# Six late experts of a mixture of experts: placed by index in 512-row units, or by token count in units of 352, 320 and 512 rows

## The chip, the cores and the metric

The kernel runs on one core of a Trainium2 chip. The metric is the device time of one execution in microseconds, as a median over runs.

## What is computed

Attention with a threshold, then a top-1 mixture of experts on its output. The attention of 8 batches and 8 heads over 576 positions gives 4608 tokens of 512 values. Each token goes to the one of 8 experts with the largest logit, and the expert's output is scaled by two gates:

```python
logits = x @ w_gate                      # x: (4608, 512), w_gate: (512, 8)
e_idx = np.argmax(logits, axis=1)
...
for e in range(E):
    mask = e_idx == e
    h = np.maximum(x[mask] @ w1[e], 0.0)  # w1[e]: (512, 1024)
    ye = h @ w2[e]                        # w2[e]: (1024, 512)
    out[mask] = gate_w[mask, None] * eom[mask, e, None] * ye
```

How many tokens each expert has is data. Counted from the reference on its own inputs, experts 0 to 7 have 619, 496, 677, 491, 670, 499, 508 and 648.

## The kernel before

**Attention** (`Attention`) runs first, with TensorE (PE), VectorE (DVE) and ScalarE (ACT) all near full. While it runs, `Router.route` finds the expert of each token, one batch pair at a time, and `Router.scatters` writes each token's row (512 values, its gate, its token number) to its place in the DRAM buffer `xs`, where every expert has a region of its own. The rows that units will read are filled beforehand from `zrow` (`init_units`), whose token number is out of range, so that an unused row writes nothing.

**The expert stage** (`Experts.run`) is a row of 12 units, written out at build time. A unit is a block of rows of one expert: experts 0 and 1 (the early ones) have 384 rows, which hold only tokens of the first three batch pairs, and run while the last batch pair is still being routed. Experts 2 to 7 (the late ones) have 512 rows each, and four `Pair` units of 256 rows stand between them for what is over. The order is E0, E1, E2, E3, pair, E4, pair, E5, pair, E6, pair, E7. Beside the fourth pair one tile of 128 rows (`Flex`) is computed, and whatever is still over goes through a loop at the end (`rest`), one tile of 128 rows at a time. Which expert a pair, the single tile and the loop's tiles take is found on chip: `Router.finish` counts what is over, and `table` makes `prows` (pairs) and `rows` (tiles), from which SP loads registers (`where`).

**Within a unit** each of 8 steps f does 12 matmuls of the first layer (`first`: weights stationary, the unit's N rows moving, lines 1065 to 1067, in three terms of a high and a low part) and then, one step behind, three matmuls for each tile of up to 128 rows in the second layer (`second`, `tile_step`: rows stationary, 512 columns of w2 moving, lines 1091 to 1093). ACT makes `hh` (line 1070) and DVE `hl` (line 1071) between the two. Weights come in chunks of two steps, four chunks for each unit; ACT and DVE split them (lines 858 and 861), and four raw buffers are refilled by SP as they come free (`load_next`).

**A unit's rows** are fetched by SP (`gather`, `fetch`, line 832) into `xg`, which has one buffer, then turned by DVE (line 1046), and split by ACT and DVE (lines 858 and 861) into `xh` and `xl`. For unit 2, the first late one, the gather has to wait for all rows of the last batch pair: its nine scatters, and then eight pad scatters (`finish`, line 698), all on GpSimd's queue (POOL, line 551), where the outputs are scattered too (line 849).

**What sets the order.** PE, DVE and ACT run in the order in which the program is written. The routing is a generator, and `rt.advance` takes it from one `yield` to the next at fixed places: four times in each step of unit 0, twice in each later step. In the expert stage POOL and SP get their order from a scheduler.

The lines of the routing that the change touches (648 to 671, then the loop of the nine scatters) are these:

```python
        nc.gpsimd.tensor_tensor(pso, pos, oh, op=ALU.mult)
        yield "V"
        split = bp <= self.cut and self.early
        dsti = t2("dsti", I32)
        V.tensor_reduce(dst, pso, axis=AX.X, op=ALU.add)
        ...
            V.tensor_copy(dsti, dst)
        ...
        for b in range(n):
```

Of the kernel before, what the change touches and what calls it, by code (L numbers as in the profile page):

```python
# [16 lines left out]
P = 128  # L17
# [434 lines left out]
class Router:  # L452
    NPAIR = 4

    def __init__(self, ctx, tc, ntok, E, DM, early, esize, cut):
# [4 lines left out]
        self.base = [esize if e < early else 4 * P for e in range(E)]  # L460
# [49 lines left out]
        self.prows = c.tile([1, 2, self.NPAIR], I32, name="pairs")  # L510
        self.total = c.tile([1, 1], I32, name="total")
# [15 lines left out]
    def init_units(self):  # L527
        E = self.E
        parts = [(self.xs[self.A :, :], "itok")]
        for e in range(self.early, E + 1):  # L530
            n = self.base[e] if e < E else 2 * P
            parts.append((self.xs[e * self.CAP : e * self.CAP + n, :], "itok"))
        for dst, group in parts:
            for r in range(0, dst.shape[0], P):
                ins = self.nc.sync.dma_start(dst[r : r + P, :], self.zrow)
                self.nodep(ins, group)
                self.behind(ins)
                self.init.append(ins)
                yield False
# [96 lines left out]
    def scatters(self, bp, rows, oh, sc, pr):  # L636
# [12 lines left out]
        yield "V"  # L649
        split = bp <= self.cut and self.early  # L650
# [35 lines left out]

    def finish(self, ctx):
# [16 lines left out]
        V.tensor_tensor(nf, self.cnt[0:1], self.ebase[0:1], op=ALU.subtract)  # L704
# [9 lines left out]
        yield from self.table(sm, "p", self.prows, cp, 2 * P, self.ebase[0:1])  # L714
# [5 lines left out]
        V.scalar_tensor_tensor(v, m0, float(2 * P), self.ebase[0:1], op0=ALU.mult, op1=ALU.add)  # L720
# [45 lines left out]
class Experts:  # L766
    RB, NW, YB = 4, 4, 4
    PAIRS = (2, 4, 6, 8)
# [56 lines left out]
    def fetch(self, xg, keys, src, after):  # L825
# [4 lines left out]
        parts.append((keys, src[:, self.rt.DM :].rearrange("(t p) w -> p t w", p=P)))  # L830
# [3 lines left out]
    def emit_out(self, y, keys, n):  # L834
        nc, DM = self.nc, self.rt.DM
        yo = self.yp.tile([P, DM], F32, name="yo")
        sc = keys[:, n, 0:1]
# [9 lines left out]
        else:  # L847
# [3 lines left out]
            out_offset=bass.IndirectOffsetOnAxis(ap=keys[:, n, 1:2].bitcast(I32), axis=0),  # L851
# [29 lines left out]
    def begin(self, nstatic):  # L881
        rt = self.rt
        make = [lambda e=e: Base(self, e) for e in range(rt.E)]
        for s, at in enumerate(self.PAIRS):
            make.insert(rt.early + at, lambda s=s: Pair(self, s))
# [7 lines left out]
        self.nload = self.done = self.used = 0  # L893
# [43 lines left out]
    def run(self):  # L937
        rt, nun = self.rt, len(self.make)
        prev, fin = None, False
        for i in range(nun):  # L940
            b, final = self.unit(i), i == nun - 1
            late = 4 if i == rt.early - 1 else 0
            for f in range(8):
# [17 lines left out]
                if not (final and f == 7):  # L961
                    if prev:
                        prev[0].second(prev[1], prev[0] is self.unit(nun - 1))
# [47 lines left out]
class Base:  # L1011
    def __init__(self, ex, e):
        self.ex, self.nc, self.e = ex, ex.nc, e
        self.nt = ex.rt.base[e] // P
        self.reset()

    def reset(self):
        self.N = self.nt * P
        self.Y, self.h, self.w = None, {}, {}

    def gather(self):
        ex, rt, e = self.ex, self.ex.rt, self.e
        early = e < rt.early
        r0 = rt.A + e * rt.esize if early else e * rt.CAP
        after = [x for g, x in rt.tok if g == "A" or not early]
        if not early:
            after += rt.pads
        else:
            assert sum(g == "A" for g, _ in rt.tok) == 9 * (rt.cut + 1)
# [54 lines left out]
    def tile_step(self, t, f, i):  # L1084
# [3 lines left out]
        n = Y.shape[1]  # L1088
        wh, wl = (w[:, f % 2, i * n : i * n + n] for w in (w2h, w2l))
        ts = slice(t * P, t * P + P)  # L1090
# [4 lines left out]
    def last(self, f0, f1):  # L1095
        for t, Y in enumerate(self.Y):
# [3 lines left out]
            self.ex.emit_out(Y, self.keys, t)  # L1100

    def finish(self):
        for t, Y in enumerate(self.Y):
            self.ex.emit_out(Y, self.keys, t)
# [9 lines left out]
class Pair(Base):  # L1114
    def __init__(self, ex, s):
        self.ex, self.nc = ex, ex.nc
        self.nt = 2
        assert "p" in ex.rt.tables
        self.e, self.row = where(ex, ex.rt.prows, s)
        self.reset()  # L1120

    def gather(self):
        rt = self.ex.rt
        self.fetch(rt.xs[bass.ds(self.row, self.N), :], [x for _, x in rt.tok] + rt.pads)

# [166 lines left out]
```

## Time and profile before

| | us |
|---|---|
| Median of 3 runs (909.41 to 909.97) | 909.64 |
| The profiled execution | 913.79 |
| Its span, first to last instruction | 912.1 |
| PE busy | 899.3 (99%) |
| DVE busy | 692.8 (76%) |
| ACT busy | 617.6 (68%) |
| POOL busy | 338.0 (37%) |
| Mean granted clock of TensorE | 0.999 of full speed |

The profile is of one execution, which was 4.15 us longer than the median run. Matmuls are pipelined: what the profile gives as the time of one is longer than the distance to the next, so a busy PE says nothing of its pace. The pace is read from the starts of matmuls that follow one another.

### The profile page before, as it was taken

How to read it: one execution, taken by the hardware profiler on the slowest of the kernel's cores; microseconds unless marked ns; L12 is line 12 of the kernel's file. 1: busy time of each engine (PE TensorE's matmuls, PEld its weight loads, DVE VectorE, ACT ScalarE, POOL GpSimd, SP SyncE). 2: the span in 40 equal slices, each digit the busy share in tenths (PEclk: the TensorE clock that was granted, in tenths of full speed). 3: DMA queues.
4: the chain of work that ended last, by engine and by line, in shares of the span. 5: the costliest groups of instructions: out<-in, count | busy, mean ns of one | idle time of the engine just before them, and what ended most of it. 6: DMA issues, size and time to landing. Idle time of an engine off the chain costs nothing.

```text
span 912.1 us, 22576 instructions
## 1 busy us (share of the span) xinstructions
PE 899.3 (99%) x8649; PEld 660.0 (72%) x8649; DVE 692.8 (76%) x1646; ACT 617.6 (68%) x1265; POOL 338.0 (37%) x529
## 2 busy tenths in 40 slices
PE   8999999999999999999999999999999999999997
PEld 4666666666666666666678978888888888888885
DVE  7999999999999999999987764545745645656821
ACT  6999999999999999999974343424434434435711
POOL 4354454656746577476656410101101101101101
PEclk9999999999999999999999999999999999999999
DMA  5477651333413334133258973527537537728401
GB/s 169 154 243 223 213 176 67 114 115 115 161 59 114 113 110 166 61 114 134 95 143 268 287 186 115 183 93 225 187 96 228 178 103 218 204 88 244 160 22 47
DMA packets 92206, 136.68 MB, mean 150 GB/s; under 512 B 14527, under 2 KB 61247, under 8 KB 92096
## 3 DMA queue, kind: packets, MB, share of 16 engines
q1 hardware_dynamic: 85456, 114.20, 41.0%
q0 software_dynamic: 6640, 21.02, 6.3%
q8 instruction: 68, 1.11, 0.5%
q14 instruction: 42, 0.34, 0.1%
HBM read 105.75 MB, written 30.22 MB: 149 GB/s over the span
## 4 chain that ended last, share of the span: by engine, by line
PE 88%; ACT 5%; DVE 3%; issue 2%; DMA 1%; another core or an unknown queue 0%; POOLq 0%; POOL 0%; DVEq 0%
PE ps L160 12%; PE pr L295 9%; PE pa L295 8%; PE ph L1066 7%; PE ph L1067 7%; PE ph L1065 7%; PE py L1093 7%; PE py L1091 7%; PE py L1092 7%; PE pt L263 7%; PE pa L221 3%; PE ps L157 2%; PE pa L321 2%; ACT p L176 2%; DMA xg<-xs 1%
## 5 line engine op out<-in xcount | busy, mean ns | idle before, releaser
L188 DVE SCALAR_TENSOR_TENSOR p<-s,thr,p 128x576 f32<-128x576 f32 x288 | 230.9, 838 | 0.0
L176 ACT ACTIVATE p<-s,mn 128x576 f32<-128x576 f32 x288 | 213.8, 783 | 24.5 <-DVE s L166 21.6
L166 DVE TENSOR_SCALAR_CACHE_REDUCE s<-ps 128x576 f32<-128x576 f32 x288 | 205.8, 751 | 26.0 <-PE ps L160 14.8
L1070 ACT ACTIVATE hh<-ph 128x512 fp32r<-128x512 f32 (+3 forms) x96 | 48.4, 504 | 189.5 <-PE ph L1067 181.1
L171 POOL TENSOR_SCALAR thr<-mn,tau_sb 128x2 f32<-128x2 f32 x144 | 107.3, 745 | 175.4 <-DVE s L166 174.6
L849 POOL DMA_INDIRECT out_dram<-yo,keys x38 | 40.5, 1065 | 353.6 <-DVE yo L848 186.0
L1071 DVE SCALAR_TENSOR_TENSOR hl<-ph,hh 128x512 fp32r<-128x512 f32 (+3 forms) x96 | 54.9, 572 | 130.5 <-ACT hh L1070 129.2
L160 PE MATMUL ps<-qk 64*128 64x288 f32 x1024 | 153.6, 419 | 0.2 <-DVE s L166 0.2
L1065 PE MATMUL ph<-xh,w1h 128*128 128x512 f32 (+2 forms) x380 | 132.1, 348 | 0.6 <-ACT xh L858 0.6
L1066 PE MATMUL ph<-xl,w1h 128*128 128x512 f32 (+2 forms) x380 | 131.8, 347 | 0.5 <-DVE xl L861 0.5
L1067 PE MATMUL ph<-xh,w1l 128*128 128x512 f32 (+2 forms) x380 | 131.9, 347 | 0.0
L1091 PE MATMUL py<-w2h,hh 128*128 128x512 f32 (+1 forms) x304 | 119.2, 392 | 0.0
L1092 PE MATMUL py<-w2l,hh 128*128 128x512 f32 (+1 forms) x304 | 118.6, 390 | 0.0
L1093 PE MATMUL py<-w2h,hl 128*128 128x512 f32 (+1 forms) x301 | 118.1, 392 | 0.0
L160 PEld LDWEIGHTS ps<-qk 64*128 64x128 f32 x1024 | 88.5, 190 | 16.2 <-DVE s L166 2.1
L295 PE MATMUL pr<-PTb,vld 128*64 128x320 f32 x640 | 100.0, 442 | 0.0
L263 PE MATMUL pt<-ident,p 64*128 64x64 f32 x2288 | 95.9, 223 | 0.2
L263 PEld LDWEIGHTS pt<-ident,p 64*128 64x128 f32 x2288 | 83.1, 139 | 2.6 <-ACT PTa L278 0.7
L295 PE MATMUL pa<-PTa,vld 128*64 128x256 f32 x640 | 80.3, 387 | 1.8 <-ACT PTb L246 1.1
L861 DVE TENSOR_TENSOR w1l<-r,w1h 128x1024 fp32r<-128x1024 f32 x52 | 64.0, 1231 | 20.9 <-ACT w1h L858 15.4
L1065 PEld LDWEIGHTS ph<-xh,w1h 128*128 128x128 f32 x380 | 71.4, 188 | 11.3 <-ACT xh L858 1.1
L1066 PEld LDWEIGHTS ph<-xl,w1h 128*128 128x128 f32 x380 | 71.5, 188 | 11.0 <-DVE xl L861 0.8
(225 smaller groups left out, 1500.6 us busy)
## 6 DMA issues: line engine op xcount, KB each, us to landing
r<-in_moe_w_dram SPq DMA_DIRECT2D x104, 512.0 KB
qk<-in_qkv_dram SPq DMA_DIRECT2D x31, 928.0 KB
vld<-in_qkv_dram SPq DMA_DIRECT2D x32, 320.0 KB
xs<-zrow SPq DMA_DIRECT2D x32, 257.0 KB
xg<-xs SPq DMA_DIRECT2D x24, 256.0 KB
xg<-xs SPq DMA_DIRECT2D x16, 128.0 KB
xg<-xs SPq DMA_DIRECT2D x8, 192.0 KB
out_dram<-yo,keys POOLq DMA_INDIRECT x38
```

What stands on the lines that cost most here:

```text
L160: nc.tensor.matmul(ps[x][:, cs], q, k, start=True, stop=True)
L166: nc.vector.tensor_scalar(s, ps[a][:, c0 : c0 + S], SC, None, op0=ALU.mult, op1=ALU.min, accum_out=mn[:, a : a + 1])
L176: self.nc.scalar.activation(e, ss[a], AF.Exp, bias=mn[:, a : a + 1], scale=-1.0)
L188: nc.vector.scalar_tensor_tensor(e, s, thr[:, a : a + 1], e, op0=ALU.is_le, op1=ALU.mult, accum_out=sums[a])
L263: nc.tensor.transpose(pt[:, o : o + 64], p[hs[h], k0 : k0 + P], id_[hs[h], hs[h]])
L295: nc.tensor.matmul(pa[self.half[a], 0:N], vm[:, kb, a], PT[:, 4 * a + kb if i else self.NK - 1], start=(i == 0), stop=(i == self.NB), skip ...
L1065: nc.tensor.matmul(ph, w1h[:, c, fs], self.xh[:, c, 0:N], start=(c == 0), stop=False)
L1066: nc.tensor.matmul(ph, w1h[:, c, fs], self.xl[:, c, 0:N], start=False, stop=False)
L1067: nc.tensor.matmul(ph, w1l[:, c, fs], self.xh[:, c, 0:N], start=False, stop=(c == 3))
L1091: nc.tensor.matmul(Y, hh[:, ts], wh, start=(f == 0), stop=False)
L1092: nc.tensor.matmul(Y, hh[:, ts], wl, start=False, stop=False)
L1093: nc.tensor.matmul(Y, hl[:, ts], wh, start=False, stop=(f == 7))
```

## The change

The base of the late experts is no longer an expert by its index but a slot by its rank. On chip, once the last batch pair is counted, the six late experts are ranked by their number of tokens (`Router.ranks`). The first has 704 rows, in two units of 352; the second and the third have 672 rows, in units of 352 and 320; the other three have one unit of 512 each. One `Pair` and the `Flex` tile remain for what is over, the two early experts' rows included. The row of units is E0, E1, 352, 352, 352, 320, 352, 320, 512, 512, pair, 512: twelve again, with 256 rows fewer. The nine late slots all take their expert and their row in `xs` from a new table `order` through registers, and no late weight is loaded before that table is there. A unit may now end in a tile of 96 or 64 rows.

```diff
 class Router:
-    NPAIR = 4
+    NPAIR = 1
+    SLOTS = ((352, 352), (352, 320), (352, 320), (512,), (512,), (512,))
...
         for dst, group in parts:
-            for r in range(0, dst.shape[0], P):
-                ins = self.nc.sync.dma_start(dst[r : r + P, :], self.zrow)
+            n = dst.shape[0]
+            m, a = (P, 1) if n % P == 0 else (n // 8, 2)
+            for r in range(0, n, m * a):
+                ins = self.nc.sync.dma_start(
+                    dst[r : r + m * a, :].rearrange("(a p) w -> p a w", a=a),
+                    self.zrow[0:m, None, :].broadcast_to([m, a, self.W]),
+                )
...
         nc.gpsimd.tensor_tensor(pso, pos, oh, op=ALU.mult)
         yield "V"
+        if bp == self.cut + 1:
+            yield from self.ranks()
         split = bp <= self.cut and self.early
         dsti = t2("dsti", I32)
         V.tensor_reduce(dst, pso, axis=AX.X, op=ALU.add)
...
+    def ranks(self):
+        nc, E, e0, V, sm = self.nc, self.E, self.early, self.nc.vector, self.small
...
+        V.scalar_tensor_tensor(key, self.cnt[0:1, e0:], float(E), key, op0=ALU.mult, op1=ALU.add)
+        V.tensor_tensor(cmp, across(key), down(key), op=ALU.is_gt)
+        yield False
+        V.tensor_reduce(rank, cmp, axis=AX.X, op=ALU.add)
...
+        V.scalar_tensor_tensor(tbl[:, 1], tbl[:, 0], float(self.CAP), off, op0=ALU.mult, op1=ALU.add)
+        V.tensor_copy(self.order, tbl)
+        self.tables.append("o")
+        yield False
...
-        V.tensor_tensor(nf, self.cnt[0:1], self.ebase[0:1], op=ALU.subtract)
+        V.tensor_tensor(nf, self.cnt[0:1], self.ends, op=ALU.subtract)
...
-        make = [lambda e=e: Base(self, e) for e in range(rt.E)]
-        for s, at in enumerate(self.PAIRS):
-            make.insert(rt.early + at, lambda s=s: Pair(self, s))
+        make = [lambda e=e: Base(self, e) for e in range(rt.early)]
+        for s, n in enumerate(n for x in rt.SLOTS for n in x):
+            make.append(lambda s=s, n=n: Slot(self, s, n))
+        make.insert(self.FLEX, lambda: Pair(self, 0))
...
     def load_next(self):
-        if self.nload < len(self.seq):
+        self.due += 1
+        while self.nload < min(self.due, len(self.seq)):
             i, g = self.seq[self.nload]
+            if i is not None and i >= self.rt.early and not self.rt.tables:
+                return
             self.nload += 1
             self.raws.append(self.load(self.unit(i).e, g))
...
         wh, wl = (w[:, f % 2, i * n : i * n + n] for w in (w2h, w2l))
-        ts = slice(t * P, t * P + P)
+        ts = slice(t * P, t * P + m)
```

**What moves, first place.** DVE in unit 0, from the copy of the last batch pair's prefix sums (`pr`) to the reduction that gives each row its place (`dst`, `dsti`). `hl` belongs to the unit's steps, `w1l` and `w2l` are weights being split. Before:

```order
L631 COPY pr<-px 128x80
L861 TENSOR_TENSOR w2l<-r_1637,w2h 128x1024
L652 TENSOR_REDUCE dst<-pso 128x9
L671 CAST dsti<-dst 128x9
L1071 SCALAR_TENSOR_TENSOR hl<-ph,hh 128x384
L861 TENSOR_TENSOR w1l<-r_8529,w1h 128x1024
L1071 SCALAR_TENSOR_TENSOR hl<-ph,hh 128x384
```

Now `pr` and `w2l` are followed by nine instructions of `ranks` (from `key` to `tbl`), and then by these:

```order
L1129 SCALAR_TENSOR_TENSOR hl<-ph,hh 128x384
L917 TENSOR_TENSOR w1l<-r_8531,w1h 128x1024
L728 SCALAR_TENSOR_TENSOR tbl<-tbl,off 1x9
L729 CAST order<-tbl 1x18
L732 TENSOR_TENSOR capr<-rank,asc 1x36
L733 TENSOR_TENSOR capr<-capr,caps 1x36
L735 COPY ends<-ebase 1x2
L736 TENSOR_REDUCE ends<-capr 1x6
L737 TENSOR_TENSOR ends<-ends,ecap 1x6
L664 TENSOR_REDUCE dst<-pso 128x9
L683 CAST dsti<-dst 128x9
L1129 SCALAR_TENSOR_TENSOR hl<-ph,hh 128x384
```

`dst` has moved behind one `hl`, one split of weights and sixteen small instructions of `ranks`.

**Second place.** POOL in units 0 and 1: the scatters of the last batch pair's rows (`xs<-rows`), the pads (`xs<-zrow`) and the outputs of unit 0 (`out_dram`). Before:

```order
L644 TENSOR_TENSOR pos<-pr,cc 128x72
L646 TENSOR_TENSOR cnt<-pr,cc 128x8
L648 TENSOR_TENSOR pso<-pos,pre_148 128x72
L551 DMA xs<-rows,dsti 38912x514 x9
L551 DMA xs<-zrow,padi 38912x514 x8
L849 DMA out_dram<-yo,keys 4608x512 x34
```

and now:

```order
L654 TENSOR_TENSOR pos<-pr,cc 128x72
L656 TENSOR_TENSOR cnt<-pr,cc 128x8
L658 TENSOR_TENSOR pso<-pos,pre_148 128x72
L561 DMA xs<-rows,dsti 38912x514 x9
L905 DMA out_dram<-yo,keys 4608x512 x3
L561 DMA xs<-zrow,padi 38912x514 x8
L905 DMA out_dram<-yo,keys 4608x512 x31
```

The three output scatters of unit 0 now stand ahead of the eight pads, for which unit 2's gather waits.

**Third place.** DVE in the first steps of unit 2, behind the weights that are split for its next steps. `ci`, `inas`, `v1s` belong to the table of single tiles (`finish`), `yo` is unit 1's output. Before, that table stood in unit 1, and these rows followed one another:

```order
L861 TENSOR_TENSOR w2l<-r_8972,w2h 128x1024
L1071 SCALAR_TENSOR_TENSOR hl<-ph,hh 128x512
L848 TENSOR_SCALAR yo<-py,keys 128x512 x2
L861 TENSOR_TENSOR w1l<-r_9099,w1h 128x1024
L1071 SCALAR_TENSOR_TENSOR hl<-ph,hh 128x512
```

and now:

```order
L917 TENSOR_TENSOR w2l<-r_8998,w2h 128x1024
L782 MEMSET ci 1x1
L784 TENSOR_TENSOR ci<-ci,nf 1x1 x6
L1129 SCALAR_TENSOR_TENSOR hl<-ph,hh 128x352
L904 TENSOR_SCALAR yo<-py,keys 128x512 x2
L917 TENSOR_TENSOR w1l<-r_9099,w1h 128x1024
L784 TENSOR_TENSOR ci<-ci,nf 1x1 x2
L776 CAST total<-ci 1x1
L799 TENSOR_TENSOR inas<-sid,ci 1x352
L800 TENSOR_TENSOR inbs<-sid,ci 1x352
L801 TENSOR_TENSOR inas<-inas,inbs 1x352
L803 TENSOR_SCALAR v1s<-ci 1x8
```

Two more rows of the table (`v1s`, `inbs`) follow before the second `hl` of unit 2.

## Rows read from the trace of the kernel before

**Rows 1.** The page's part 1: busy us, share of the span, instructions.
```profile
PE 899.3 (99%) x8649; PEld 660.0 (72%) x8649; DVE 692.8 (76%) x1646; ACT 617.6 (68%) x1265; POOL 338.0 (37%) x529
```

**Rows 2.** A group of PE instructions, shapes apart (the single tile's first layer): shapes, xcount, busy us, mean ns, idle.
```profile
L1156 PE MATMUL ph<-w1h,xfh 128*128 128x256 f32 x16 | 4.5, 280 | 0.0
```

**Rows 3.** Timeline of PE, three stretches: start us, us, line, op, tiles, idle.
```profile
309.01 1.83 PE L295 MATMUL pr<-PTb,vld 128*64 128x320 f32 x12
...
515.06 0.34 PE L1065 MATMUL ph<-xh,w1h 128*128 128x384 f32 x1
...
517.15 0.40 PE L1091 MATMUL py<-w2h,hh 128*128 128x512 f32 x1
...
519.24 0.34 PE L1065 MATMUL ph<-xh,w1h 128*128 128x384 f32 x1
...
639.98 0.28 PE L1065 MATMUL ph<-xh,w1h 128*128 128x256 f32 x1
...
641.40 0.39 PE L1091 MATMUL py<-w2h,hh 128*128 128x512 f32 x1
```

**Rows 4.** Timeline of PE where unit 1 hands over to unit 2.
```profile
531.75 0.39 PE L1065 MATMUL ph<-xh,w1h 128*128 128x512 f32 x1
...
533.94 0.49 PE L1065 MATMUL ph<-xh,w1h 128*128 128x512 f32 x1 [0.65 <-ACT xh L858]
...
536.19 0.40 PE L1091 MATMUL py<-w2h,hh 128*128 128x512 f32 x1
```

**Rows 5.** Timeline of DVE at the last batch pair's routing, units 0 and 1.
```profile
483.68 0.23 DVE L652 TENSOR_REDUCE dst<-pso 128x9 f32<-128x72 f32 x1 [0.69 <-POOL pso L648]
...
485.34 1.23 DVE L861 TENSOR_TENSOR w1l<-r,w1h 128x1024 fp32r<-128x1024 f32 x1 [0.38 <-ACT w1h L858]
...
499.08 0.15 DVE L704 TENSOR_TENSOR nf<-cnt,ebase 1x8 f32<-1x8 f32 x1
...
500.43 0.15 DVE L712 CAST np<-nj 1x8 f32<-1x8 int32 x1
...
502.08 1.39 DVE L848 TENSOR_SCALAR yo<-py,keys 128x512 f32<-128x512 f32 x2
503.66 1.22 DVE L861 TENSOR_TENSOR w1l<-r,w1h 128x1024 fp32r<-128x1024 f32 x1 [0.20 <-issue]
```

**Rows 6.** Timeline of POOL: first row scatter, first pad scatter, first output scatter.
```profile
484.40 1.09 POOL L551 DMA_INDIRECT xs<-rows,dsti  x1 [0.76 <-DVE dsti L671]
...
498.22 1.78 POOL L551 DMA_INDIRECT xs<-zrow,padi  x1 [0.30 <-issue]
...
510.17 0.97 POOL L849 DMA_INDIRECT out_dram<-yo,keys  x1 [0.30 <-issue]
```

**Rows 7.** Timeline of SP: DMA issues of unit 2's gather and weights among them.
```profile
515.48 0.33 SPq L832 DMA_DIRECT2D xg<-xs  x1
515.91 0.48 SPq L807 DMA_DIRECT2D r<-in_moe_w_dram  x1
516.44 0.46 SPq L832 DMA_DIRECT2D xg<-xs  x1
516.99 1.01 SPq L807 DMA_DIRECT2D r<-in_moe_w_dram  x2
518.05 1.69 SPq L832 DMA_DIRECT2D xg<-xs  x2
```

**Rows 8.** Timeline of DVE after that gather has landed.
```profile
529.38 1.30 DVE L1046 STREAM_TRANSPOSE xt<-xg 128x512 f32<-128x512 f32 x2 [2.38 <-issue]
```

**Rows 9.** Timeline of DVE over the tables of the single tiles.
```profile
520.25 0.32 DVE L731 TENSOR_TENSOR ci<-ci,nf 1x1 f32<-1x1 f32 x2
...
522.92 0.54 DVE L1071 SCALAR_TENSOR_TENSOR hl<-ph,hh 128x384 fp32r<-128x384 f32 x1
```

**Rows 10.** Two stretches of attention: us, busy us by engine, PEclk, DMA share, GB/s.
```profile
48.60:77.20 28.60, 28.58 (x408) 18.14 (x406) 26.94 (x75) 27.18 (x62) 13.85 (x21) 1.00 0.78 248
134.40:163.00 28.60, 28.58 (x410) 18.00 (x406) 27.58 (x85) 27.29 (x64) 14.19 (x21) 1.00 0.33 116
```

More of the change, by code (lines that the diff above doesn't have):

```diff
@@ L459, in __init__ @@
         self.W = DM + 2
-        self.base = [esize if e < early else 4 * P for e in range(E)]
+        self.caps = [sum(x) for x in self.SLOTS]
+        self.base = [esize if e < early else self.caps[0] for e in range(E)]
+        assert early + len(self.caps) == E and self.caps == sorted(self.caps)[::-1]
         self.early, self.cut = early, cut
@@ L510, in __init__ @@
         self.prows = c.tile([1, 2, self.NPAIR], I32, name="pairs")
+        self.order = c.tile([1, 2, sum(len(x) for x in self.SLOTS)], I32, name="order")
+        self.ends = c.tile([1, E], F32, name="ends")
         self.total = c.tile([1, 1], I32, name="total")
@@ L713, in finish @@
         yield from self.sums(cp, np)
-        yield from self.table(sm, "p", self.prows, cp, 2 * P, self.ebase[0:1])
+        yield from self.table(sm, "p", self.prows, cp, 2 * P, self.ends)
         self.tables.append("p")
@@ L1013, in __init__, with reset, size @@
         self.ex, self.nc, self.e = ex, ex.nc, e
[L1014 to L1018, printed above, removed]
+        self.reset(ex.rt.esize)
+    def reset(self, N):
+        self.N, self.nt = N, -(-N // P)
         self.Y, self.h, self.w = None, {}, {}
+    def size(self, t):
+        return min(P, self.N - t * P)
     def gather(self):
[L1022 to L1029, printed above, removed]
+        rt = self.ex.rt
+        r0 = rt.A + self.e * rt.esize
+        after = [x for g, x in rt.tok if g == "A"]
+        assert len(after) == 9 * (rt.cut + 1)
         self.fetch(rt.xs[r0 : r0 + self.N, :], after)
@@ L1111, in where, with __init__, place @@
     return e, nc.sync.value_load(table[0:1, 1, sl], min_val=0, max_val=rt.E * rt.CAP)
-class Pair(Base):
-    def __init__(self, ex, s):
+class Slot(Base):
+    def __init__(self, ex, s, N):
         self.ex, self.nc = ex, ex.nc
[L1117 to L1120, printed above, removed]
+        self.place(s)
+        self.reset(N)
+    def place(self, s):
+        assert "o" in self.ex.rt.tables
+        self.e, self.row = where(self.ex, self.ex.rt.order, s)
     def gather(self):
@@ L1124, in gather, with __init__, place @@
         self.fetch(rt.xs[bass.ds(self.row, self.N), :], [x for _, x in rt.tok] + rt.pads)
+class Pair(Slot):
+    def __init__(self, ex, s):
+        super().__init__(ex, s, 2 * P)
+    def place(self, s):
+        assert "p" in self.ex.rt.tables
+        self.e, self.row = where(self.ex, self.ex.rt.prows, s)
 class Flex:
```

58 lines of the change are left out of this document (46 added, 12 removed).

## The prediction

> **What bounds the kernel now.** I read the page's busy shares first, then PE's timeline for the pace, then the timelines of the engines that PE waits for. PE is busy 99% of the span [rows 1], but the time given for one matmul is longer than its distance to the next, so this is no proof. The pace is: in the expert stage one 128x512 matmul starts 0.232 us after the other (9 second-layer matmuls from 517.15 to 519.24), one of 384 columns 0.174 us (12 from 515.06 to 517.15), one of 256 columns 0.118 us (12 from 639.98 to 641.40) [rows 3]. I read the timeline through all 12 units: they run at this pace with no break above 0.2 us, save at the handover from unit 1 to unit 2, where PE waits twice [rows 4]. There the first step of unit 2 has 12 matmuls from 531.75 to 536.19, 4.44 us, where the pace gives 2.79: 1.65 us lost. What it waits for is unit 2's rows, at the end of a long chain: routing of the last batch pair on DVE [rows 5], nine row scatters and eight pad scatters on POOL [rows 6], the gather on SP [rows 7], DVE's transposes [rows 8]. So the time of the expert stage is its number of matmul columns, plus what this one chain is late. The reader is to see both: a change that takes columns away pays fully, and one that makes this chain longer pays back.
>
> **Columns removed: -10.9 us.** In the first layer a unit's rows are the moving columns, 96 matmuls for each unit. The late blocks had 6 x 512 + 4 x 256 = 4096 rows and now have 4 x 352 + 2 x 320 + 3 x 512 + 256 = 3840. Between 256 and 512 columns the pace rises by 0.445 ns for a column; 384 lies on that line (0.175 against 0.174 measured), and attention's 320-column matmuls start 12 in at most 1.83 us, 0.152 us or less each, where the line gives 0.147 [rows 3]. So 256 x 96 x 0.445 ns = 10.9 us. In the second layer the rows are stationary and 512 columns move whatever their number: a tile of 96 or 64 rows costs as much as one of 128. There are 6 + 24 + 8 = 38 tiles before and 6 + 18 + 12 + 2 = 38 now: nothing.
>
> The Trainium skill (TensorE: Matmul & The Clock Gate, section "Wait — 56ns, not 53.3ns?") gives a warm matmul its columns at 2.4 GHz and about 2.5 ns on top. By that a column costs 0.417 ns, the saving would be 10.2 us, and the sum below 901.0. The trace does not agree (0.232 us for 512 columns, where the page has 0.216), so the measured pace stands.
>
> **The chain to unit 2: +0.6 us, from -1.1 to +9.0.** `ranks` is put ahead of `dst`. Its instructions are of the kind of the small ones on one partition: eight start from 499.08 to 500.43, 0.19 us apart [rows 5]. The first nine (1.7 us) take the place that `dst` leaves and the gaps in which DVE waits for POOL (0.69 us ahead of `dst`) and for ACT (0.38 us ahead of the split of weights at 485.34); they make `hl` some 0.3 us late, and the split not at all. Then come this split (1.2 us), seven more small ones (1.3 us) and `dst`, at 487.9 instead of 483.68: 4.2 us late. On POOL 17 scatters lie between 484.40 and 510.17 [rows 6], 1.52 us each. Now unit 0's three outputs stand ahead of the pads, so the last pad is 4.2 + 3 x 1.52 = 8.8 us late. (The pads' indices are made later too, behind the split at 503.66, but that is over by 505.3, and the pads' turn comes at 506.8.) The gather starts at 515.48 + 8.8 = 524.3.
>
> From its first issue to the first transpose it took 13.9 us before (515.48 to 529.38 [rows 7, 8]), with 4 parts of 256 KB and, among them, three weight loads of 512 KB. Now the parts have 176 KB, and the weight loads of that time are out before them, since the gather is late. By the bytes alone this is 13.9 x 704 / 2560 = 3.8 us, by the row as it stands 13.9. I take 5.5, near the bytes, with room for the four issues: the first transpose starts at 529.8 (528.1 to 538.2). From there to the end of the first step it was 6.8 us; transposing and splitting 352 columns instead of 512 takes some 1.4 us off, and seven small instructions instead of three put 0.7 back: 6.1, so 535.9. Without a wait PE would be there at 531.75 + 12 x 0.161 = 533.7. It loses 2.2 us instead of 1.65: +0.6. The ends are 0.5 us lost (-1.1) and 10.6 (+9.0).
>
> **The table of single tiles: +0.8 us, from 0 to 2.** `finish` runs later, so the tables for the single tile fall into unit 2, just when DVE has come late out of the handover. From the end of unit 2's `xl` to the second `hl` DVE has three splits of weights (1.2 each), six sums (1.0, by the two at 520.25), two `hl` (0.5 each), two outputs (1.4) and the table (520.25 to 522.92, 2.7): 9.7 us [rows 5, 9]. PE gets to where it needs that `hl` after the rest of its first step (0.35), two second-layer steps of 9 matmuls (2.1 each), two first-layer steps (1.9 each) and two matmuls (0.5): 8.9. It waits 0.8. The steps after that have 4.0 us for some 3.6 us of DVE work and catch up. Below nothing it can't go: no wait of PE stands where the table was.
>
> **The zero fills: +0.2 us, from 0 to 20.** 24 of the 32 fills grow from 128 to 176 rows. While they run, the DMA engines' share is 0.78 (48.60 to 77.20), later 0.33 (134.40 to 163.00), and PE is busy 28.58 of 28.60 us in both [rows 10]: attention doesn't notice. The nearest row is that, so I take almost nothing, and a gain is excluded, since bytes are only added. If the whole difference of 0.45 doubled, the share would be 1.23, 6.6 us too much in each such stretch, 20 over three. The Trainium skill speaks against these fills (DMA: Bandwidth & Descriptors, section "Why a DMA increments its semaphore by 16 and not by 1"): a DMA from SP spreads over the largest number of engines up to 16 that divides its slowest dimension, so 128 partitions go to 16 engines and the new 88 to 11. A fill would then take about twice as long; no run here shows it.
>
> **At nothing.** SP's 18 register loads from `order` and the weight loads behind them: `order` is there at about 487.3, when the split of 485.34 has just freed the raw buffer for the first late chunk, and that chunk is split some 30 us later. Without that cover a late chunk would cost PE its whole delay. POOL's ten more fills of single values, and a sixth DMA in each gather, which has 20 us from one unit's first step to the next transposes.
>
> **The sum.** -10.9 + 0.6 + 0.8 + 0.2 = -9.3 us. The profiled execution took 913.79 us, so 904.5; it was 4.15 us over the median of the runs, so 900.3 against 909.64.
>
> **Rivals.** (a) The gather takes as long as before, since queue and receipts and not bytes make it slow. For: 13.9 us is the only row there is. Against: weight loads and outputs shared that time. Up to 8.4 us more, 903 to 908.7. (b) The gather lands before PE is there: no wait, and DVE ahead again: 897 to 898.5. (c) Columns are paid in steps of 128, so that 352 and 320 cost as 384 (0.174 us): 6 x 96 x 0.174 = 100.3 us instead of 90.0, and the time is 910.6. All units of the expert stage so far are multiples of 128; attention's 320 columns speak against it [rows 3]. (d) A late expert has more tokens than its slot, and the loop at the end runs once. The counts, taken from the reference, are 677, 670 and 648 for 704, 672 and 672 rows, and 508, 499 and 491 for 512; the early experts' 235 and 112 rows over take the pair and the single tile. It decides at the 673rd token of the second expert, three more than there are: an iteration shares nothing with other work, so at least a gather (13.9 us) and eight splits of weights (1.2 us each), 24 us: 924, slower than before. That the routing on chip gives such counts the trace shows in part: a single tile ran beside the units, and no more (16 matmuls of line 1156, four for each of its four weight chunks [rows 2]). (e) The fills take so much longer that attention's loads come late: up to 920, slower too. It decides where the DMA share passes 1; 0.78 with 353 KB in place of 257 KB doesn't reach that.
>
> **How the numbers follow.** The forecast has 0.68, 898.5 to 903; (a) 0.16, (b) 0.06, (c) 0.04, (d) 0.03, (e) 0.03. The range 897.0 to 905.0 takes in the forecast, (b) and the nearer half of (a): 0.82. A difference of 0.2%, 1.8 us, is about what can be told from no change. Faster by more (under 907.8): the forecast, (b) and nearly all of (a), 0.89. Within 0.2%: the end of (a) and (c), 0.05. Slower: (d) and (e), 0.06.
>
> **What the profile after would show.** First-layer matmuls of 352 columns at a pace of 0.161 us and of 320 columns at 0.147; 38 tiles in the second layer. First row scatter near 488.6, last pad near 519, gather issue near 524, first transpose near 530, PE's idle there near 2.2 us, and one more wait of PE for `hl` in unit 2's second step. Attention ends as before. I am wrong if the pace of 352 columns is that of 384, if unit 2 starts after 538, if PE shows new waits in later units, or if line 1156's successor shows more than 16 matmuls.

## The result and the profile after

| | before | after |
|---|---|---|
| Median, us (4 runs each) | 909.81 (909.41 to 911.47) | 900.66 (900.56 to 900.76) |
| The profiled execution | 913.79 | 900.56 |
| Its span | 912.1 | 898.8 |
| First matmul of unit 0 to last of the last unit | 465.62 to 905.15 | 463.29 to 892.30 |

The ratio is 0.9896, with a 95% interval of 0.9879 to 0.9913: about 1.0% faster. The forecast was 900.3, with a range of 897.0 to 905.0.

The page's busy shares of after, beside [rows 1]: PE has 12.5 us less, the other engines are within 4 us of where they were.

```profile
PE 886.8 (99%) x8649; PEld 656.0 (73%) x8649; DVE 693.7 (77%) x1665; ACT 613.6 (68%) x1262; POOL 341.2 (38%) x539
```

PE's timeline (start us, us, line, op, tiles, idle and what ended it) at the handover to unit 2, and at the first step of a unit of 320 rows. In `after`, lines 1123 to 1125 are the first layer, 1150 to 1152 the second, 1129 is `hl`.

```profile
529.50 0.32 PE L1123 MATMUL ph<-xh,w1h 128*128 128x352 f32 x1
...
531.79 0.42 PE L1123 MATMUL ph<-xh,w1h 128*128 128x352 f32 x1 [1.17 <-ACT xh L914]
...
532.57 0.43 PE L1124 MATMUL ph<-xl,w1h 128*128 128x352 f32 x1 [0.35 <-DVE xl L917]
...
533.47 0.39 PE L1150 MATMUL py<-w2h,hh 128*128 128x512 f32 x1
...
535.57 0.32 PE L1123 MATMUL ph<-xh,w1h 128*128 128x352 f32 x1
...
537.47 0.39 PE L1150 MATMUL py<-w2h,hh 128*128 128x512 f32 x1
...
539.54 0.32 PE L1123 MATMUL ph<-xh,w1h 128*128 128x352 f32 x1
...
542.66 0.50 PE L1152 MATMUL py<-w2h,hl 128*128 128x512 f32 x1 [0.55 <-DVE hl L1129]
542.99 0.39 PE L1150 MATMUL py<-w2h,hh 128*128 128x512 f32 x1
...
632.33 0.31 PE L1123 MATMUL ph<-xh,w1h 128*128 128x320 f32 x1
...
634.09 0.39 PE L1150 MATMUL py<-w2h,hh 128*128 128x512 f32 x1
```

The first 12 matmuls of unit 2 take from 529.50 to 533.47, 3.97 us, where its second step takes 1.90 for the same 12 (535.57 to 537.47, 0.158 each) and the forecast pace of 0.161 gives 1.93: by the latter 2.04 us are lost, as two waits, for `xh` and `xl`. In [rows 4] it was 1.65. Then 542.66 comes late: a matmul that waits for `hl`. From 539.54 to the next start, 542.99, there are 12 matmuls of the first layer and three of the second, 2.63 us by the pace, in 3.45: 0.82 us are lost. Those are the only breaks of PE above 0.15 us in the stage. Twelve matmuls of 320 columns take 1.76 (632.33 to 634.09, 0.147 each). The nine second-layer matmuls from 537.47 to 539.54, three of them with a tile of 96 rows, take 2.07, 0.230 each, within a hundredth of the 0.232 of tiles of 128.

The chain ahead of it, on DVE, POOL and SP, and DVE again, beside [rows 5 to 9]. Unit 0 starts 2.33 us earlier here than in the profile of before, so that 2.33 has to be added to compare.

```profile
485.17 0.21 DVE L664 TENSOR_REDUCE dst<-pso 128x9 f32<-128x72 f32 x1
...
485.87 1.09 POOL L561 DMA_INDIRECT xs<-rows,dsti  x1 [4.58 <-DVE dsti L683]
...
500.72 0.97 POOL L905 DMA_INDIRECT out_dram<-yo,keys  x1 [1.70 <-DVE yo L904]
...
514.76 0.97 POOL L561 DMA_INDIRECT xs<-zrow,padi  x1 [0.30 <-issue]
...
522.05 1.90 SPq L887 DMA_DIRECT2D xg<-xs  x4
...
527.75 0.97 DVE L1104 STREAM_TRANSPOSE xt<-xg 128x352 f32<-128x352 f32 x2 [3.22 <-DMA xg<-xs]
...
530.69 0.95 DVE L1104 STREAM_TRANSPOSE xt<-xg 128x352 f32<-128x352 f32 x2
...
542.10 0.51 DVE L1129 SCALAR_TENSOR_TENSOR hl<-ph,hh 128x352 fp32r<-128x352 f32 x1
```

`dst` stands behind the ranking, at 485.17. The three outputs (from 500.72) stand ahead of the eight pads (the first at 505.08, the last at 514.76), and the gather is issued at 522.05. 5.70 us later the first transpose starts. Between it and the second tile's, at 530.69, stand seven small instructions; the second `hl` of unit 2 is made at 542.10.

A stretch of attention, beside the first of [rows 10], and one at the end of unit 1 (columns: us, busy us of PE, PEld, DVE, ACT, POOL, then PEclk, DMA share, GB/s):

```profile
48.60:77.20 28.60, 28.58 (x410) 18.14 (x408) 26.93 (x75) 27.17 (x62) 13.87 (x21) 1.00 0.84 262
524.00:529.60 5.60, 5.60 (x29) 4.93 (x28) 2.25 (x5) 1.27 (x3) 0.00 (x0) 1.00 1.12 260
```

And the single tile's first layer, beside [rows 2]: 16 matmuls, so the loop at the end didn't run.

```profile
L1226 PE MATMUL ph<-w1h,xfh x16: 276/280/283, 817.4 to 843.1; 128*128 128x256 f32 x16
```

### The profile page after: what moved, and what is told of

Same layout as the page of the kernel before. It is cut to its first block, busy times and chain, and to the rows that moved or that the text cites. A ratio compares the mean times of both kernels' runs of the same rounds, so it can differ in the third digit from the quotient of the medians.

```text
span 898.8 us, 22802 instructions
## 1 busy us (share of the span) xinstructions
PE 886.8 (99%) x8649; PEld 656.0 (73%) x8649; DVE 693.7 (77%) x1665; ACT 613.6 (68%) x1262; POOL 341.2 (38%) x539
## 5 line engine op out<-in xcount | busy, mean ns | idle before, releaser
L1128 ACT ACTIVATE hh<-ph 128x352 fp32r<-128x352 f32 (+5 forms) x96 | 46.8, 487 | 193.6 <-PE ph L1125 193.1
L905 POOL DMA_INDIRECT out_dram<-yo,keys x38 | 45.2, 1190 | 335.9 <-DVE yo L904 209.7
L1129 DVE SCALAR_TENSOR_TENSOR hl<-ph,hh 128x352 fp32r<-128x352 f32 (+5 forms) x96 | 52.8, 550 | 122.4 <-ACT hh L1128 122.1
L1123 PE MATMUL ph<-xh,w1h 128*128 128x352 f32 (+4 forms) x380 | 128.4, 338 | 1.2 <-ACT xh L914 1.2
L1124 PE MATMUL ph<-xl,w1h 128*128 128x352 f32 (+4 forms) x380 | 128.0, 337 | 0.4 <-DVE xl L917 0.4
L1125 PE MATMUL ph<-xh,w1l 128*128 128x352 f32 (+4 forms) x380 | 128.1, 337 | 0.0
L1150 PE MATMUL py<-w2h,hh 128*128 128x512 f32 (+3 forms) x304 | 119.2, 392 | 0.0
L1151 PE MATMUL py<-w2l,hh 128*128 128x512 f32 (+3 forms) x304 | 118.7, 391 | 0.0
L1152 PE MATMUL py<-w2h,hl 128*128 128x512 f32 (+3 forms) x301 | 117.7, 391 | 0.6 <-DVE hl L1129 0.6
L1123 PEld LDWEIGHTS ph<-xh,w1h 128*128 128x128 f32 x380 | 71.4, 188 | 10.2 <-ACT xh L914 1.5
L917 DVE TENSOR_TENSOR w2l<-r,w2h 128x1024 fp32r<-128x1024 f32 x52 | 64.1, 1235 | 18.1 <-ACT w2h L914 17.7
## 6 DMA issues: line engine op xcount, KB each, us to landing
xs<-zrow SPq DMA_DIRECT2D x24, 353.4 KB
```

Of the source, the lines that this page charges most:

```text
L917: self.nc.vector.tensor_tensor(lo, src, hi, op=ALU.subtract)
L1123: nc.tensor.matmul(ph, w1h[:, c, fs], self.xh[:, c, 0:N], start=(c == 0), stop=False)
L1124: nc.tensor.matmul(ph, w1h[:, c, fs], self.xl[:, c, 0:N], start=False, stop=False)
L1125: nc.tensor.matmul(ph, w1l[:, c, fs], self.xh[:, c, 0:N], start=False, stop=(c == 3))
L1150: nc.tensor.matmul(Y, hh[:, ts], wh, start=(f == 0), stop=False)
L1151: nc.tensor.matmul(Y, hh[:, ts], wl, start=False, stop=False)
```

## The experiments

The result left four questions. Is the profile of before, 4 us over its median, a fair thing to make the sum against? Is the column term the whole gain? Which of the parts of the delay (the ranking, the outputs that go ahead, the table) costs what? And what do the rivals on the loop and the fills cost in truth? The table gives every kernel's median, its ratio to the kernel before timed with it, and where the profiled execution's expert stage lies.

| kernel | median us | ratio, 95% interval | profiled us | stage from, to | length |
|---|---|---|---|---|---|
| before (the profile shown) | 909.81 | | 913.79 | 465.62, 905.15 | 439.53 |
| before again | 909.88 (one) | | 909.88 | 463.46, 901.28 | 437.82 |
| after | 900.66 | 0.9896 (0.9879 to 0.9913) | 900.56 | 463.29, 892.30 | 429.01 |
| ranking behind the scatters | 897.46 | 0.9861 (0.9845 to 0.9878) | 897.87 | 463.44, 889.59 | 426.15 |
| ranking in one go | 897.92 | 0.9871 (0.9855 to 0.9888) | 897.91 | 463.49, 889.64 | 426.15 |
| table early | 901.84 | 0.9910 (0.9893 to 0.9926) | 901.99 | 462.92, 893.70 | 430.78 |
| one more pad | 904.55 | 0.9918 (0.9904 to 0.9933) | 905.88 | 465.28, 897.51 | 432.23 |
| four more pads | 906.00 | 0.9956 (0.9939 to 0.9972) | 906.68 | 463.56, 898.62 | 435.06 |
| 384 and 384 rows | 908.50 | 0.9987 (0.9977 to 0.9996) | 908.47 | 463.16, 900.23 | 437.07 |
| loop runs once | 916.12 | 1.0072 (1.0056 to 1.0089) | 915.88 | 462.55, 887.38 | 424.83 |
| fills from 22 partitions | 902.09 | 0.9893 (0.9878 to 0.9908) | 903.60 | 465.48, 895.27 | 429.79 |
| fills from 16 partitions | 918.16 | 1.0089 (1.0072 to 1.0105) | 921.82 | 485.52, 913.56 | 428.04 |
| fills from 11 partitions | 953.99 | 1.0456 (1.0439 to 1.0474) | 956.38 | 519.11, 948.04 | 428.93 |

The kernels with one more pad and with fills from 22 and from 11 partitions were timed where the kernel before had a median of 911.70 to 911.92, 2 us more than elsewhere: their ratios are to be read, not their microseconds.

### The kernel before, once more

No edit.

> The kernel before again, for a second profiled execution of it. The first was 4.15 us over the median, and lost about 2.3 us in attention against the kernel after (465.62 against 463.29 at the first matmul of unit 0). If the loss is chance of that one execution, this one ends near 909.8 with attention ending near 463.3 and, from the first to the last matmul of the expert stage, 439.5 as before; then the change gave 10.5 in the expert stage and lost or gained about 1.4 elsewhere. If the longer attention belongs to the kernel before, this one is near 913 again.

SP, DVE and PE of this execution, at the handover to unit 2:

```profile
512.81 0.33 SPq L832 DMA_DIRECT2D xg<-xs  x1
...
525.16 1.30 DVE L1046 STREAM_TRANSPOSE xt<-xg 128x512 f32<-128x512 f32 x2 [0.54 <-DMA r<-in_moe_w_dram]
...
529.60 0.39 PE L1065 MATMUL ph<-xh,w1h 128*128 128x512 f32 x1
...
532.38 0.40 PE L1091 MATMUL py<-w2h,hh 128*128 128x512 f32 x1
```

It ended at 909.88, with attention ending at 463.46, so the longer attention of the first profile doesn't belong to the kernel before: the profile of the kernel with one more pad shows the same 2 us in attention (465.28), on an occasion on which the kernel before took 2 us more too. But the expectation's second half fell. The stage took 437.82 and not 439.53, since PE doesn't wait here at all: the first step of unit 2 takes 2.78 us (529.60 to 532.38), the bare pace. The gather took 12.35 us (512.81 to 525.16) where [rows 7, 8] have 13.9, and DVE waits 0.54 us ahead of its first transpose where it waited 2.38. So of the 3.9 us by which the first profile was longer, 2.2 lie in attention and 1.7 at this handover, and this execution, which lies at the median, loses nothing there. It is one execution: how often the kernel before loses the 1.7 is not known.

### The ranking behind the scatters

```diff
-        if bp == self.cut + 1:
-            yield from self.ranks()
+        ranks = self.ranks() if bp == self.cut + 1 else iter(())
...
             self.tok.append(("A" if split else "B", self.scatter(r, dsti[:, b : b + 1], "tok")))
+            next(ranks, None)
             yield "S"
```

> The kernel after, with the ranking on DVE put behind the nine scatters, one piece behind each, instead of ahead of the reduction that gives the rows their place. So the scatters start some 4.2 us earlier, the pads stand ahead of unit 0's outputs on POOL again, and the table of the single tiles is back in unit 1. Theory: the gather comes about 9 us earlier than in the kernel after, PE loses nothing at the handover to unit 2 (2.04 less) and no wait for hl in its second step (0.82 less): about 897.8. Rival: the earlier gather falls among the loads of weights again and takes near the 13.9 us of the kernel before, so that the rows come no earlier: about 900.7. Second rival: the slots' table comes later, so the late weights load later, and the handover waits for weights instead: 900.7 or more.

POOL's first row scatter and last pad, SP's queue, DVE at the first transpose, and PE over the first step of unit 2:

```profile
482.42 1.09 POOL L561 DMA_INDIRECT xs<-rows,dsti  x1 [0.97 <-DVE cmp L716]
...
506.76 0.97 POOL L561 DMA_INDIRECT xs<-zrow,padi  x1 [0.31 <-issue]
...
478.75 35.41 SPq L859 DMA_DIRECT2D r<-in_moe_w_dram  x10
...
514.64 1.38 SPq L887 DMA_DIRECT2D xg<-xs  x3
...
524.59 0.96 DVE L1104 STREAM_TRANSPOSE xt<-xg 128x352 f32<-128x352 f32 x2
...
529.65 0.32 PE L1123 MATMUL ph<-xh,w1h 128*128 128x352 f32 x1
...
531.56 0.39 PE L1150 MATMUL py<-w2h,hh 128*128 128x512 f32 x1
```

897.46 against 897.8 expected. The stage is 2.86 us shorter than in `after`, which is the two waits, 2.04 and 0.82: PE goes through the first step of unit 2 in 1.91 us (529.65 to 531.56), and no wait for `hl` follows. The first row scatter is 3.6 us earlier measured from the stage's start (482.42 against 485.87, with 0.15 between the starts), the last pad 8.2. How long the gather takes can't be read, since DVE's first transpose has no idle time ahead of it; it is at most 9.95 us (514.64 to 524.59). SP's row shows why the gather gains 7.6 and not the 8.2 of the last pad: ahead of it stand weight loads that wait until 514.2 for a raw buffer.

### The ranking in one go

```diff
     def ranks(self):
...
-        yield False
```

All six `yield False` are taken out, so that the sixteen instructions run in one piece, still ahead of `dst`.

> The kernel after, with the ranking still ahead of the reduction that gives the rows their place, but written out in one go instead of over seven places in the program, so that nothing else moves: the pads stand ahead of unit 0's outputs again, and the single tile's table is back in unit 1. What is left of the delay is the ranking's own sixteen small instructions, some 3.0 us ahead of the first row scatter. Theory (the handover's 2.04 came of the outputs that went ahead, and the chain has some us of slack): no wait at the handover, 897.5, or up to 1.5 more if hl in unit 0 comes late. Rival (the chain has no slack): the gather is 3 us late and PE with it, about 900.5.

POOL's first row scatter and SP's gather:

```profile
484.61 1.09 POOL L561 DMA_INDIRECT xs<-rows,dsti  x1 [3.09 <-DMA r<-in_moe_w_dram]
...
514.93 0.87 SPq L882 DMA_DIRECT2D xg<-xs  x2
```

897.92, and the same stage length, 426.15. The row scatters start 2.1 us later than with the ranking behind (484.61 against 482.42), the last pad 1.3 (508.08 against 506.76), but the gather only 0.2, since it stands behind the same weight loads on SP's queue. So the ranking's own instructions cost nothing. What cost `after` 2.86 us is only that they were spread over seven places of the program: everything behind them, the pads and the tables, slid to later places, the pads behind three outputs. How the 2.04 at the handover divides between the later rows and the three outputs no run separates; on POOL's queue the outputs alone take 4.4 us (500.72 to 505.08 in `after`).

### The table early

```diff
-                for _ in range((3 if f == 0 else 4) if i == 0 else 2):
+                for _ in range((3 if f == 0 else 4) if i == 0 else 3 if i == 1 else 2):
```

> The kernel after, with the routing advanced three times instead of twice in each step of unit 1, so that the table of the single tiles is done in unit 1 and no longer in unit 2; the chain to unit 2's rows and POOL's order stay. Theory: only the wait for hl in unit 2's second step (0.82) goes: about 899.9. Rival: the table's small instructions cost the same wherever they stand, as DVE then is late in unit 1: 900.7. Second rival: it brings the pads earlier too and takes part of the handover's 2.04: down to 897.9.

DVE between the two tiles' transposes, PE's wait, and the stretch behind it:

```profile
528.64 0.50 DVE L807 TENSOR_REDUCE slfs<-inbs 1x44 f32<-1x352 f32 x1
...
531.24 0.95 DVE L1104 STREAM_TRANSPOSE xt<-xg 128x352 f32<-128x352 f32 x2
...
532.34 0.43 PE L1123 MATMUL ph<-xh,w1h 128*128 128x352 f32 x1 [2.09 <-ACT xh L914]
...
533.40:537.50 4.10, 4.10 (x14) 3.39 (x14) 3.56 (x5) 2.12 (x4) 0.00 (x0) 0.58 0.36 105
```

901.84, 1.2 us slower than `after`; none of the three expectations saw that. The wait for `hl` is indeed gone. The first tile's transpose comes even 0.72 us earlier (526.66 against 527.75, with starts of 462.92 and 463.29). But now eight of the table's instructions, four of them of 0.50 us (528.64 and on), stand between the first tile's split and the second tile's transpose, which comes 0.92 us later measured from the stage's start (531.24 against 530.69), and PE waits 2.09 us for `xh` instead of 1.17. Behind that wait TensorE's granted clock is 0.58 over 4.1 us, near 0.50, the lower of its two levels (1.2 GHz against 2.4): 512-column matmuls start 0.43 us apart where they start 0.232 apart at a clock of 1.00. The same stretch of `after`:

```profile
533.40:537.50 4.10, 4.10 (x24) 3.69 (x23) 3.87 (x11) 2.64 (x4) 0.97 (x1) 1.00 0.49 151
```

So +0.92 of wait, -0.82 for `hl`, and the rest of the +1.77 of stage, 1.67 us, is the clock. Why the clock falls behind this wait and not behind that of `after`, no run shows.

### Four more pads, one more pad

```diff
-        for e in range(E):
+        for e in [*range(E), *range(4)]:
```

The second kernel has `[*range(E), 0]`. The pads that are written twice change nothing in the output.

> The kernel after, with four of the eight pad scatters made twice, so that twelve stand ahead of unit 2's gather on POOL. Theory (the chain through POOL sets when unit 2 can run, and has no slack): four scatters of 1.3 to 1.5 us each make the handover 5.2 to 6.0 us later: about 906. Rival (the chain has slack, and the 2.04 lost at the handover is for another reason, the weights of unit 2): about 900.7.

> The kernel after, with one of the eight pads scattered twice. Theory A (the chain sets the handover one to one, and nothing else happens): one scatter of 1.28 us, 901.9, and PE's wait for hl in unit 2's second step stays. Theory B (a wait of PE for xh of 2.09 us was followed by some 4 us at half clock where four or one of 1.17 us was not): the wait for xh is near 2.4 us, the granted clock falls to 0.5 behind it for some us, which costs 1.6 us, and the wait for hl of 0.82 is gone, since PE itself comes later: 902.7.

With four more, DVE's first transpose, PE's wait, and two stretches behind it:

```profile
532.58 0.97 DVE L1104 STREAM_TRANSPOSE xt<-xg 128x352 f32<-128x352 f32 x2 [7.79 <-DMA xg<-xs]
...
533.70 0.66 PE L1123 MATMUL ph<-xh,w1h 128*128 128x352 f32 x1 [3.77 <-ACT xh L914]
...
533.60:538.00 4.40, 3.65 (x9) 2.55 (x10) 3.99 (x15) 2.78 (x7) 0.00 (x0) 0.50 0.28 101
538.00:542.30 4.30, 4.30 (x13) 3.65 (x12) 4.07 (x11) 1.82 (x3) 0.00 (x0) 0.50 0.47 140
```

906.0, as the chain's theory had it, but not by its sum. The first transpose is 4.56 us later than in `after` (532.58 against 527.75, starts 463.56 and 463.29), the wait for `hl` (0.82) is gone, and the stage is 6.05 longer: 2.3 us net are left over, and the granted clock of 0.50 over two stretches says where they are. With one more pad, PE's two waits and a stretch behind them:

```profile
532.37 0.43 PE L1123 MATMUL ph<-xh,w1h 128*128 128x352 f32 x1 [0.71 <-ACT xh L914]
...
535.29 0.66 PE L1123 MATMUL ph<-xh,w1h 128*128 128x352 f32 x1 [1.29 <-ACT xh L914]
...
537.50:541.50 4.00, 4.00 (x11) 3.21 (x10) 3.48 (x11) 1.52 (x4) 0.04 (x1) 0.51 0.62 180
```

The first transpose is 1.51 later (531.25 against 527.75, starts 465.28 and 463.29) and the stage 3.22 longer, so with the 0.82 gone 2.5 us are the clock's. Theory B's one wait near 2.4 came as two, and the clock falls during the second (0.81 over 534.00 to 535.00, 0.50 from there). By the ratio the time is 902.3, between the two theories (901.9 and 902.7), and the runs scatter from 902.39 to 906.38: the profile decides for the clock, the time doesn't. The clock doesn't fall in every execution either: its mean is 0.999 in the two shortest of these five runs and 0.994 to 0.997 in the three longest. Another kernel's execution shows half clock behind a wait that is nearly that of `after`: the profiled one of the kernel with fills from 22 partitions, whose second-layer matmuls start 0.43 us apart from 536.12 on, and which is the longest of that kernel's four runs (mean clock 0.996, in the other three 0.998 and 0.999):

```profile
533.97 0.43 PE L1123 MATMUL ph<-xh,w1h 128*128 128x352 f32 x1 [1.15 <-ACT xh L914]
...
536.10:539.40 3.30, 3.30 (x10) 2.60 (x9) 3.07 (x11) 1.85 (x4) 0.39 (x1) 0.50 0.47 156
```

### 384 and 384 rows

```diff
-    SLOTS = ((352, 352), (352, 320), (352, 320), (512,), (512,), (512,))
+    SLOTS = ((384, 384), (384, 384), (384, 384), (512,), (512,), (512,))
```

The base is the kernel with the ranking behind the scatters, so that no wait stands in the way.

> The kernel with the ranking behind the scatters (897.46, no wait of PE at the handover), with two units of 384 rows for each of the three largest experts in place of 352 and 352 or 320: 256 rows more in the first layer, as many tiles in the second. Theory (a column costs 0.445 ns at any number of columns): 256 x 96 x 0.445 ns = 10.9 us more, 908.4. By 0.417 ns a column, 10.2 more, 907.7. Rival (columns are paid in steps of 128, so that 352 and 320 cost what 384 do): no change, 897.5.

908.50, 11.0 us more; the stages differ by 437.07 - 426.15 = 10.92 us. Over 256 x 96 columns that is 0.444 ns each. The rival with steps of 128 columns is out, and 0.417 ns a column, 10.2 us, with it. The 0.417 is an estimate from the 2.4 GHz at which the Trainium skill (TensorE: Matmul & The Clock Gate, section "Wait — 56ns, not 53.3ns?") lets a warm matmul take its columns; the trace does not agree, here a column of these matmuls costs 0.444.

### The loop runs once

```diff
-    SLOTS = ((352, 352), (352, 320), (352, 320), (512,), (512,), (512,))
+    SLOTS = ((352, 352), (352, 320), (320, 320), (512,), (512,), (512,))
```

> The kernel with the ranking behind the scatters (897.46), with 320 and 320 rows for the third largest expert, whose 648 tokens then pass its 640 rows by eight, so that the loop at the end runs once. Theory: 32 x 96 x 0.445 ns = 1.4 us less of columns, and one iteration of the loop that shares nothing with other work, at least 24 us (a gather and eight splits of weights, one after the other): 920 or more. Rival: the loop's loads are out early enough that only its matmuls and its output count, some 8 us: about 904.

DVE's first transpose of the loop, behind the last unit's last matmul at 887.38, and a stretch of the loop:

```profile
889.32 0.89 DVE L1215 STREAM_TRANSPOSE xt<-xgf 128x128 f32<-128x128 f32 x4 [0.87 <-DVE yo L900]
...
893.40:898.40 5.00, 5.00 (x24) 5.00 (x25) 4.46 (x5) 2.94 (x5) 0.00 (x0) 0.50 0.00 0
```

916.12: with the 1.3 us that the stage is shorter (1.4 expected), the loop's one iteration costs 20.0 us, not 24 or more. The gather is not in it: SP issued it at 843.93, beside the last units' work, and DVE turns its rows 1.9 us after the last matmul. Nor are the splits of weights the rest. From the last unit's last matmul to the loop's first (891.86) there are 4.5 us of transposes and first splits; then PE is busy almost without a break from 893.12 to 906.35, and over the first 5 us of that at a granted clock of 0.50 (256-column matmuls start 0.213 us apart, where they have 0.118 at 1.00), behind an idle time of 4.2 us.

### The zero fills from fewer partitions

```diff
-            m, a = (P, 1) if n % P == 0 else (n // 8, 2)
+            m, a = (P, 1) if n % P == 0 else (16, n // 64)
```

The other two have `(n // 32, 8)`, 22 partitions, and `(11, n // 44)`. Each moves the same 353.4 KB in a fill, from 88 partitions in `after`.

> The kernel after, with each zero fill of 176 rows written from 16 partitions, eleven rows each, instead of from 88 partitions, two rows each. The Trainium skill (DMA: Bandwidth & Descriptors, section on why a DMA increments its semaphore by 16) spreads the one over 16 engines and the other over 11. Theory: attention doesn't notice the fills in either form: 900.7, with attention's marks where they are; the DMA share between 48.6 and 77.2 stays at 0.84, since the bytes are the same. Rival (fills on fewer engines hold up attention's loads): the share and the time fall by some tenths of a us.

> The kernel after, with each zero fill of 176 rows written from 22 partitions, eight rows each. By the Trainium skill's rule (DMA: Bandwidth & Descriptors, section on why a DMA increments its semaphore by 16) 22 partitions spread over 11 engines, as the 88 of the kernel after do, while the 16 partitions that cost 17.5 us spread over 16. Theory A (the number of partitions that the rows are read from sets the time of a fill): near the 16 partitions, fills of some 7 to 9 us and 912 to 918. Theory B (the number of engines sets it): as the kernel after, 900.7.

> The kernel after, with each zero fill of 176 rows written from 11 partitions, sixteen rows each. From 88 and from 22 partitions a fill costs attention nothing, from 16 it costs 17.5 us. Theory A (sixteen engines reading one partition each is the slow case; eleven engines, as 22 and 88 partitions use by the Trainium skill's rule, leave attention's loads room): 900.7, a ratio to the kernel before of 0.990. Theory B (fewer partitions make the fill slower, with the edge between 22 and 16): worse than 16, 918 or more, a ratio of 1.009 or more.

Fills from 16 partitions: two stretches of attention, one of SP's issues, and from the table of DMA issues (KB each, median us from issue to landing) the fills and attention's loads over 20 to 170:

```profile
48.60:77.20 28.60, 28.58 (x412) 18.20 (x410) 26.94 (x75) 27.17 (x63) 13.86 (x20) 1.00 0.90 206
77.20:105.80 28.60, 23.49 (x274) 14.48 (x272) 20.83 (x57) 20.86 (x47) 9.54 (x15) 0.94 0.94 207
...
116.58 4.04 SPq L99 DMA_DIRECT2D qk<-in_qkv_dram  x1
...
xs<-zrow SPq DMA_DIRECT2D x24, 353.4 KB, 9.5
qk<-in_qkv_dram SPq DMA_DIRECT2D x9, 928.0 KB, 11.2
```

The issue that takes SP 4.04 us here takes 0.36 in `after` (at 114.98).

Fills from 22 partitions, one stretch:

```profile
77.20:105.80 28.60, 28.57 (x408) 18.13 (x408) 26.94 (x75) 27.19 (x62) 13.87 (x21) 1.00 0.77 242
```

Fills from 11, the same stretch, and PE's longest wait (us in total, times, longest):

```profile
77.20:105.80 28.60, 15.25 (x194) 9.75 (x190) 13.15 (x36) 12.85 (x34) 5.29 (x8) 0.76 0.72 145
...
PE ps L160 <- DMA qk<-in_qkv_dram: 16.6, 2, 13.3
```

From 22 partitions the fills cost nothing, from 16 they cost 17.5 us, from 11 about 50 (0.0560 of 909.8, the difference of the ratios, is 51 us). Attention's loads of `qk` come late: 11.2 us to landing with 16, where the second execution of before has 6.0 over the same stretch. PE waits for them, and its granted clock is below 1.00 as well (0.94, 0.88 and 0.88 in the three stretches of 28.6 us from 77.20 on), so the 17.5 us are idle time and clock together. The Trainium skill (DMA: Bandwidth & Descriptors, section "Why a DMA increments its semaphore by 16 and not by 1") gives 16 engines to 16 partitions and 11 to 88, 22 and 11; no trace here shows the number of engines. The order of the times, 88 and 22, then 16, then 11, doesn't follow that number; it follows the number of partitions that the rows are read from. Why fewer partitions are slow, and whether it is a step between 22 and 16 or a slope, was not tried.

## Why the prediction was right

The time came out within 0.4 us of the forecast, and its mechanism was the one that happened. Step by step:

- **What bounds the kernel.** Right: every kernel with a wait of PE removed or added in the expert stage moved by that wait, or by more where the granted clock fell with it, which the prediction had not, and where no wait is left PE has no break above 0.2 us in the stage.
- **Columns, -10.9.** Right: 10.92 measured by itself, 0.158 to 0.160 us for 352 columns, 0.147 for 320, and a tile of 96 rows at the price of 128.
- **The chain.** Right in its places: the first row scatter was expected 4.2 us late and was 3.8 (485.87 + 2.33 against 484.40 of [rows 6]), the gather 8.8 and was 8.9, gather to transpose 5.5 and was 5.7 (5.7 to 5.8 in all seven kernels in which DVE waits for it), transpose to the end of the first step 6.1 and was 5.7, PE's loss 2.2 and was 2.04. Rival (a) was wrong: out of the way of the weight loads, and with 704 KB for 1024, the gather took less than half as long. Which of the two did it, no run separates.
- **The table, +0.8.** Right, 0.82 at the place named. No other break came, so what was put at nothing cost nothing.
- **Fills, +0.2.** Nothing measured: attention's marks have a period of 28.4 us in both kernels. But rival (e) was judged by the wrong thing. It was to decide where the mean DMA share passes 1. At a share of 0.72 PE stood idle for 13 of 28.6 us with fills from 11 partitions, and at 1.12 (524.00 to 529.60 in `after`) it was busy all the time. What kept attention clear was the form of the fills, 88 partitions (22 do as well), where the prediction's sum went by bytes alone.
- **The loop, 24 or more.** Mis-sized: 20.0, and near only by luck: the gather that was in the sum is hidden, and PE's own matmuls, in part at half clock, which were not in it, take its place.
- **The sum.** Here the working failed, and the number was saved by luck, by small things on the other side. The chain's term was made against the 1.65 us that [rows 4] lose, as +0.6, and then the whole 4.15 us by which that execution exceeded the median was taken off. But 1.7 of those were that loss itself, so it was taken off twice. Against the second execution of before (909.88, no loss) the steps give -10.9 + 2.2 + 0.8 + 0.2 = -7.7, 902.2. That is 1.6 more than the profiled 900.56. Of these, 0.5 is three breaks of PE of 0.15 to 0.18 us each where a pair of 256 rows handed over to a unit of 512 in the kernel before (648.6, 715.8 and 783.0 in the first profile, and as long in the second), which are gone with the pairs and which the prediction saw as "no break above 0.2"; 0.2 is the fills, and 0.2 the handover. The other 0.75 us lie 0.2 ahead of the stage, 0.2 within it and 0.3 behind it, and no run here says why.

So the change is worth 10.9 us in columns, of which it gives back 2.9 by its place in the program. With the ranking behind the scatters, or in one go, those come back: 897.46, 0.9861 of the kernel before, is the best version here.

## What to carry to other kernels

A step that is spread over places in an emission order shifts everything behind it: before pricing its own instructions, list what slides, on which queue, and past what. When a profile is longer than the median, find where its excess lies before taking it off a sum, since a wait that the change removes or remakes may be part of it. And price a change in rows or columns by the pace of matmuls that follow one another, at the size that they will have, then look for the one wait that can give it back.

## What was not expected of the hardware

- A wait of PE can cost more than its length. Behind waits of 2.09 and 0.35 us, or already during those of 0.71 and 1.29 and of 3.77, the granted clock fell to about half (0.50 to 0.58 over 4 us and more), worth 1.7, 2.5 and 2.3 us net; behind 1.17 and 0.35 it stayed at 1.00 (`after`), behind 1.15 and 0.36 in another kernel's execution it fell to 0.50 (fills from 22 partitions).
- The number of partitions that a DMA reads its rows from can matter more than its bytes: 353.4 KB from 88 or 22 partitions passed unseen beside attention, from 16 the fill took 9.5 us to land and SP 4 us to issue the next load, and the kernel lost 17.5 us.
- The mean DMA share of a stretch says little of whether loads come late: 0.72 with PE idle half the time, 1.12 with PE full.
- A gather in four parts of 176 KB took 5.7 us with SP's queue clear, one in four parts of 256 KB 12.4 and 13.9 with three weight loads issued among its parts: more than the bytes grow by.
